# Which of a pair's two products with K gets which PSUM bank, in a fused attention kernel

## The chip, the cores and the metric

The kernel runs on one core of a Trainium2 chip. The metric is the device time of one execution in microseconds (us). The kernel before takes 1962.55 us (median of 3 runs, 1960.83 to 1966.76).

The engines in this text: PE is TensorE (PEld its weight loads), ACT is ScalarE, DVE is VectorE, POOL is GpSimd, SP issues most transfers. PE writes its results into PSUM, which has eight banks of 128 x 512 fp32 elements.

## What is computed

Two attention blocks read the same input x (2048 tokens, width 512, 32 heads of 16) and are mixed by a gate. Block A is causal within each of four segments of 512 tokens and adds a memory of the segments before; block B is full attention over 2048 keys.

```python
x = A_x
g = _sigmoid((x * gate_w).sum(-1, keepdims=True))
a = _A_ref(x, A_wq, A_wk, A_wv, A_wo, A_beta)
b = _B_ref(x, B_wqkv, B_wo)
return g * a + (1 - g) * b
...
scores = jnp.einsum("bhqd,bhkd->bhqk", q, k) * (Dh ** -0.5)
p = _softmax(scores, axis=-1)
o = jnp.einsum("bhqk,bhkd->bhqd", p, v)
...
logits = jnp.einsum("bhqd,bhkd->bhqk", qs, ks) * scale + mask
p = _softmax(logits, axis=-1)
a_dot = jnp.einsum("bhqk,bhkd->bhqd", p, vs)
```

## The kernel before

The first 336 us project q, k and v, build A's memory and begin with the running maxima. Then come 32 passes (the loop over `k`, line 919), one for each set of four heads and 512 queries. Each pass handles one unit of B (16 blocks of 128 keys) and one unit of A (4 blocks of 128 keys, below and on the diagonal).

**Groups.** A pass is cut into 37 groups (the loop over `n`, line 922): 32 for B, two heads of one key block each, then 5 for A. A group is one call of `t_group` (line 502) and consists of

- two products with K (line 514), one for each of two heads. Their results are 128 keys x 512 queries and each fills one PSUM bank. The two heads lie in rows 0 to 63 and 64 to 127, so that PE runs the two products side by side. A's last three groups have four smaller products, two in each bank;
- two exponentials on ACT (line 520), in the order of the products. Exponential `j` reads bank `bs[j]` whole and writes the probabilities to `raw`; for A, POOL then clears what lies above the diagonal (line 523).

**Banks.** `bank` (line 87) returns, of the banks that it may use, the one whose last *call* is longest ago. It keeps a list of calls and knows nothing of products or readers. `t_group` calls it twice (line 506). In passes 0 to 30 it may use three banks: two named `tb` and one named `mb`; so the calls of successive groups go A B, C A, B C, and so on. In pass 31 two more banks (`sbk`) are allowed. Twice in a pass another user takes a bank out of the same three: `m_rows` (line 483, the transposition of the maxima, PE line 487, behind group 24) and, from pass 9 on, `out_mm` (line 598, twelve products of the output projection, PE line 602, in group 1; pass 31 has a second one).

**The order of the work.** The schedule is written by hand, and each engine runs its instructions in the order of the program. Between the products of one group and those of the next, PE runs: the products for the running maxima of a later unit (`s_b`, line 453, two products into an `sbk` bank, read by a DVE reduction, line 462; or `s_a`, line 428, for A), and half of the products with V of the key block before (`pv`, line 526, eight products in most groups, all into bank `pvb`). In pass 0 groups 0, 2, 4 and 6 also hold one projection job each (`qk_job`, line 285). Behind the last group of every second pass from pass 8 on, ACT copies four blocks of the output (`out_split`, line 594). Results leave `pvb` once for each unit (`fin_copy`, line 539), and the divisions and the output follow in the next pass. Transfers are issued by SP in the order of the program.

Of the kernel before, what the change touches and what calls it, by code (L numbers as in the profile page):

```python
# [34 lines left out]
def gated_mix_kernel(ctx, tc, xt, wq, wk, wv, wo, beta, wqkv, wob, gate_w, out):  # L35
# [51 lines left out]
    def bank(allowed):  # L87
        b = min(allowed, key=lambda a: max([n for n, x in enumerate(lru) if x is a], default=-1))
        lru[:] = [x for x in lru if x is not b] + [b]
        return b  # L90
# [295 lines left out]
    def q_of(u):  # L386
        return QA[u % 2] if u < 32 else QB[u % 3]

    def k_of(u, p):
        return KA[u % 2][:, p] if u < 32 else KB[(u - 32) % 3][:, p]  # L390
# [111 lines left out]
    def t_group(u, n, banks):  # L502


        kd, qd, c = UN[u]
        bs = [bank(banks) for _ in range(2)]
        c0 = 0
        for it, hs in (((n // 2, (n % 2 * 2, n % 2 * 2 + 1)),) if kd == "B" else GA[n]):
            q0 = 128 * it if kd == "A" else 0
            w = C - q0  # L510
            pn = it if kd == "B" else it % 2
            for j, h in enumerate(hs):
                r = slice(64 * j, 64 * j + 64)
                nc.tensor.matmul(bs[j][:, c0:c0 + w], k_of(u, h // 2)[r, 128 * it:128 * it + 128],  # L514
                                 q_of(u)[r, h // 2, q0:], start=True, stop=True)
                PT[u, it, h] = PTILE[pn % 2][:, 2 + j if (kd, it) == ("A", 2) else h][:, c0:c0 + w]
            c0 += w
        for j in range(2):
            pt = PTILE[pn % 2][:, 2 + j if (kd, n) == ("A", 4) else hs[j]]
            nc.scalar.activation(pt, bs[j], AF.Exp, scale=SCALE)  # L520
            if kd == "A":
                m = pt[:, :128] if n < 2 else pt.rearrange("p (a t) -> p a t", a=4)[:, ::3 if n < 4 else 2]
                nc.gpsimd.affine_select(out=m, in_=m, pattern=[[1, 128]] if n < 2 else [[0, 2], [1, 128]],  # L523
                                        compare_op=OP.is_ge, fill=0.0, base=0, channel_multiplier=-1)
# [394 lines left out]
    for k in range(32):  # L919
        ua, ub = k, 32 + k  # L920
        banks = T3 + [b[:, 0] for b in SBK] * (k == 31)
        for n in range(NG):
            it = n // 2 if n < NG - 1 else NT + 2
            t_group(*(ub, n) if n < 2 * NT else (ua, n - 2 * NT), banks)
            for f in plan.get((k, n), []) + ex[k][0].get(n, []):
                f()
# [82 lines left out]
```

## Time and profile before

| | before |
|---|---|
| time, median of 3 runs | 1962.55 us |
| time of the profiled execution | 1963.14 us |
| its span, first to last instruction | 1961.4 us |
| busy: PE, DVE, ACT, POOL | 99%, 83%, 73%, 14% |
| mean granted clock of PE | 0.998 |
| first product of pass 0, of pass 31 | 336.7 us, 1890.3 us |

The profile belongs to one execution. A row of a group list gives line, engine, operation, output<-input, shapes and count; behind the bar the busy time in us, the mean of one in ns, the idle time of the engine before these instructions and what ended most of it. A row of the waits gives who waited for whom, the total in us, the number of waits and the longest. A row of the timeline gives start and length in us, engine, line, operation and names, the count where neighbours are merged, and in brackets the idle time of the engine before it and what ended it. Buffer numbers are left out of names, so both banks `tb` read as tb. A row of the chain that ended last gives start, length, engine and line. PE's ends are modelled, since matmuls are pipelined.

### The profile page before, as it was taken

The page shows a single profiled execution, that of the slowest core. Times are in us where ns is not written, and L with a number is a line of the kernel's source. Part 1 is how long each engine was busy: PE and PEld are TensorE (multiplying, and loading weights), DVE is VectorE, ACT ScalarE, POOL GpSimd, SP SyncE. Part 2 cuts the span into 40 slices and gives each one's busy share as a digit, 9 for nine tenths or more (in the row PEclk, how much of TensorE's full clock was granted, in tenths as well). Part 3 has the DMA queues.
Part 4 walks back from the last instruction along what each step waited for, and adds up shares of the span by engine and source line. Part 5 has one row for each costly group of instructions (what it writes and reads, how often), then busy time and mean ns, then how long its engine had stood idle before and what let it go on. Part 6 is the DMA issues. An engine that isn't in the chain of part 4 may idle for free.

```text
span 1961.4 us, 43525 instructions
## 1 busy us (share of the span) xinstructions
PE 1938.5 (99%) x17485; PEld 942.3 (48%) x17485; DVE 1629.3 (83%) x1800; ACT 1433.3 (73%) x2699; POOL 268.6 (14%) x483
## 2 busy tenths in 40 slices
PE   8999999999999999999999999999999999999999
PEld 6887776444344444444444444444444444444445
DVE  6135765899999999999999999999999999999942
ACT  4233332688888888888888888888888888888884
POOL 4101000012120101111111111010101010101022
PEclk9999999999999999999999999999999999999999
DMA  7666656644443445343444443445444443434111
GB/s 221 170 195 195 194 187 179 154 98 114 97 115 90 108 90 107 82 111 81 115 87 114 87 114 86 113 86 114 87 107 95 107 95 88 101 88 107 48 50 58
DMA packets 163534, 222.23 MB, mean 113 GB/s; under 512 B 39788, under 2 KB 90428, under 8 KB 157572
## 3 DMA queue, kind: packets, MB, share of 16 engines
q1 hardware_dynamic: 159284, 211.41, 43.4%
q0 software_dynamic: 2992, 7.77, 2.1%
q8 instruction: 138, 2.26, 0.5%
q14 instruction: 64, 0.52, 0.1%
q10 hardware_dynamic: 1056, 0.26, 0.1%
HBM read 147.95 MB, written 68.16 MB: 110 GB/s over the span
## 4 chain that ended last, share of the span: by engine, by line
PE 95%; DVE 3%; ACT 1%; DMA 0%; SPq 0%; issue 0%; DVEq 0%; ACTq 0%
PE pvb L536 33%; PE tb L514 17%; PE sbk L460 12%; PE mb L514 9%; PE tb L290 4%; PE sbk L438 3%; PE tb L602 2%; PE mb L290 2%; PE sbk L273 1%; PE tb L273 1%; PE sbk L442 1%; PE pvb L290 1%; DVE mxb L462 1%; PE mb L602 1%; PE mb L273 1%; PE pvb L273 1%
## 5 line engine op out<-in xcount | busy, mean ns | idle before, releaser
L462 DVE TENSOR_REDUCE mxb<-sbk 128x2 f32<-128x1024 f32 x1024 | 1222.1, 1222 | 69.3 <-PE sbk L460 65.0
L520 ACT ACTIVATE raw<-tb 128x512 f32<-128x512 f32 x1555 | 887.6, 598 | 157.2 <-PE tb L514 81.7
L536 PE MATMUL pvb<-raw,vb 128*17 128x256 f32 (+1 forms) x8072 | 639.3, 388 | 0.0
L520 ACT ACTIVATE raw<-mb 128x512 f32<-128x512 f32 x782 | 467.9, 598 | 81.0 <-PE tb L514 38.3
L514 PE MATMUL tb<-qb,xh 64*128 64x512 f32 x872 | 331.1, 494 | 1.7 <-ACT raw L520 1.7
L536 PEld LDWEIGHTS pvb<-raw,vb 128*17 128x17 f32 x8072 | 134.4, 95 | 341.6 <-issue 336.5
L460 PE MATMUL sbk<-xh,qb 64*128 64x512 f32 x1344 | 281.7, 396 | 4.5 <-DMA xh<-dB 2.6
L514 PE MATMUL mb<-qb,xh 64*128 64x512 f32 x445 | 220.5, 495 | 0.0
L523 POOL TENSOR_SCALAR_AFFINE_SELECT raw<-raw 128x256 f32<-128x256 f32 (+1 forms) x320 | 115.5, 361 | 713.0 <-ACT raw L520 705.0
L514 PEld LDWEIGHTS tb<-qb,xh 64*128 64x128 f32 x872 | 124.5, 183 | 179.6 <-issue 90.1
L514 PE MATMUL tb<-qb,kb 64*128 64x512 f32 x470 | 179.4, 495 | 1.3 <-DVE st L300 0.8
L446 DVE TENSOR_REDUCE mx<-sbk 128x2 f32<-128x768 f32 (+1 forms) x128 | 136.7, 1090 | 25.2 <-PE sbk L442 19.2
L460 PE MATMUL sbk<-kb,qb 64*128 64x512 f32 x704 | 146.3, 398 | 0.0
L460 PEld LDWEIGHTS sbk<-xh,qb 64*128 64x128 f32 x1344 | 138.7, 186 | 9.0 <-DVE mxb L462 4.3
L514 PEld LDWEIGHTS mb<-qb,xh 64*128 64x128 f32 x445 | 81.3, 183 | 95.2 <-issue 50.4
L514 PEld LDWEIGHTS tb<-qb,kb 64*128 64x128 f32 x470 | 68.2, 183 | 100.1 <-issue 53.1
L514 PE MATMUL mb<-qb,kb 64*128 64x512 f32 x234 | 116.0, 496 | 0.0
L576 POOL TENSOR_TENSOR o<-o,d 128x512 f32<-128x512 f32 x31 | 39.8, 1283 | 548.9 <-DMA d<-rd 486.0
L536 PE MATMUL pvb<-raw,va 128*17 128x256 f32 (+2 forms) x1280 | 94.7, 384 | 0.8 <-ACT pvs L545 0.8
L438 PE MATMUL sbk<-ka,qa 64*128 64x256 f32 (+3 forms) x512 | 89.8, 358 | 0.3
L297 ACT ACTIVATE st<-tb 128x512 fp32r<-128x512 f32 x33 | 19.7, 598 | 84.4 <-DVE phi L296 49.1
L514 PE MATMUL tb<-qa,ka 64*128 64x512 f32 (+3 forms) x339 | 79.6, 372 | 0.0
(280 smaller groups left out, 1839.8 us busy)
## 6 DMA issues: line engine op xcount, KB each, us to landing
xh<-dB SPq DMA_DIRECT2D x38, 512.0 KB
vb<-vdB SPq DMA_DIRECT2D x16, 1088.0 KB
dB<-st SPq DMA_DIRECT2D x64, 256.0 KB
dA<-st SPq DMA_DIRECT2D x64, 256.0 KB
pd<-pvs SPq DMA_DIRECT2D x64, 256.0 KB
kb<-dB SPq DMA_DIRECT2D x22, 512.0 KB
xh<-dB SPq DMA_DIRECT2D x38, 256.0 KB
qb<-dB SPq DMA_DIRECT2D x64, 128.0 KB
```

The lines of the kernel that those rows point to most:

```text
L273: nc.tensor.matmul(b, lhs, WV[wi][:, k, :], start=n == 0, stop=n == 11)
L290: nc.tensor.matmul(b, WS[ws][w][wi][:, k, :], (XH, XL)[xi][c][:, k, :], start=n == 0, stop=n == 11)
L438: nc.tensor.matmul(b[:, j, c0:c0 + n], q_of(u)[r, p, i * 128:(i + 1) * 128], k_of(u, p)[r, :n], start=True, stop=False)
L446: nc.vector.tensor_reduce(m[:, :, p, i], b[:, :, :n], axis=AX.X, op=OP.max)
L460: nc.tensor.matmul(b[:, j], q_of(u)[r, p, i * 128:(i + 1) * 128], k_of(u, p)[r, kc * C:(kc + 1) * C], start=True, stop=True)
L462: nc.vector.tensor_reduce(MXB[u][:, :, p, i, kc], b, axis=AX.X, op=OP.max)
L514: nc.tensor.matmul(bs[j][:, c0:c0 + w], k_of(u, h // 2)[r, 128 * it:128 * it + 128], q_of(u)[r, h // 2, q0:], start=True, stop=True)
L520: nc.scalar.activation(pt, bs[j], AF.Exp, scale=SCALE)
L523: nc.gpsimd.affine_select(out=m, in_=m, pattern=[[1, 128]] if n < 2 else [[0, 2], [1, 128]], compare_op=OP.is_ge, fill=0.0, base=0, channe ...
L536: nc.tensor.matmul(PVB[32 * h:32 * h + E + 1, q0 + lo:q0 + hi], vt[:, it, 4 * q + h, :], pt[:, lo:hi], start=it == 0 and lo == 0, stop=it ...
L576: nc.gpsimd.tensor_tensor(o, o, d, op=OP.mult)
L602: nc.tensor.matmul(b, (AT["oh"], AT["ol"])[oi][:, g, a], (AT["wh"], AT["wl"])[wi][:, g, a], start=n == 0, stop=n == 11)
```

## The change

One line of `t_group` is changed. `bank` is called twice as before, in the same order, and the list of the two banks is then reversed: the first product and the first exponential use the bank of the second call, the second product and the second exponential the bank of the first call. All 1184 calls of `t_group` do so. Nothing else is touched.

```diff
@@ -503,7 +503,7 @@


         kd, qd, c = UN[u]
-        bs = [bank(banks) for _ in range(2)]
+        bs = [bank(banks) for _ in range(2)][::-1]
         c0 = 0
         for it, hs in (((n // 2, (n % 2 * 2, n % 2 * 2 + 1)),) if kd == "B" else GA[n]):
             q0 = 128 * it if kd == "A" else 0
```

## The prediction

> **What bounds the kernel now.** I read the page's totals first, then the list of waits, then the timeline of a few groups, then the chain that ended last over one whole pass. "Product" below means a product with K (line 514), "exponential" the ACT instruction of line 520 that reads its bank.
>
> ```profile
> span 1961.4 us, 43525 instructions
> PE 1938.5 (99%) x17485; PEld 942.3 (48%) x17485; DVE 1629.3 (83%) x1800; ACT 1433.3 (73%) x2699; POOL 268.6 (14%) x483
> L462 DVE TENSOR_REDUCE mxb<-sbk 128x2 f32<-128x1024 f32 x1024 | 1222.1, 1222 | 69.3 <-PE sbk L460 65.0
> L520 ACT ACTIVATE raw<-tb 128x512 f32<-128x512 f32 x1555 | 887.6, 598 | 157.2 <-PE tb L514 81.7
> ```
>
> PE is busy 99% of the span, ACT 73%, and one exponential takes 598 ns. That alone would say: PE sets the time and ACT has room. The list of waits says how little room:
>
> ```profile
> PEld tb L514 <- ACT raw L520: 155.4, 371, 0.6
> PEld mb L514 <- ACT raw L520: 77.2, 182, 0.9
> ```
>
> 553 weight loads of products already have ACT's release as the last one. (The idle time in these rows counts the weight loader, which also idles while the products with V stream, so it is no PE loss.) The timeline shows the rotation. An "x2" row merges neighbours: the exponential of 1002.86 ends 0.59 later, at 1003.45, and the next one starts at 1003.53.
>
> ```profile
> 1001.77 0.18 PEld L514 LDWEIGHTS mb<-qb,xh 64*128 64x128 f32 x1 [0.42 <-issue]
> 1001.78 0.18 PEld L514 LDWEIGHTS tb<-qb,xh 64*128 64x128 f32 x1
> ...
> 1002.37 0.60 ACT L520 ACTIVATE raw<-mb 128x512 f32<-128x512 f32 x1 [0.22 <-PE tb L514]
> ...
> 1002.86 1.26 ACT L520 ACTIVATE raw<-tb 128x512 f32<-128x512 f32 x2
> 1003.00 0.18 PEld L514 LDWEIGHTS tb<-qb,xh 64*128 64x128 f32 x1 [0.42 <-ACT raw L520]
> ...
> 1003.02 0.18 PEld L514 LDWEIGHTS mb<-qb,xh 64*128 64x128 f32 x1
> ```
>
> The group at 1001.77 writes mb, then tb. Its first exponential reads mb until 2.97, its second reads tb until 3.45. The next pair starts at 3.00 with the other tb bank, which is free, and its second product enters mb at 3.02, 0.05 us after mb was read. So today a pair waits for the **first** exponential of the group before, and PE gets there 0.03 us after that exponential ends. The second exponential ends 0.45 us after the pair has started, and nobody waits for it. This overlap, the next pair under the second exponential, holds the period at PE's own length.
>
> **The change, part by part.** It adds and removes no instruction and no transfer; it exchanges the two banks of each call. The order in which the rotation hands out banks stays, because it follows the calls. With calls (A, B), (C, A), (B, C), the first product takes B, then A, then C. Bank A was in the group before the bank of the second product, since that exchange was made there too, so the **second** exponential read it. The second product gets a bank whose reader ended a group earlier.
>
> The wait is thus moved, from the end of exponential 1 to the end of exponential 2, and from the pair's second product to its first. Behind that product stand, in PE's order, its partner, the two products of the running maxima (line 460), the eight with V (line 536) and the next pair. DVE's reductions wait for the maxima, ACT waits for the pair itself. So product, exponential 1, exponential 2 and the next product become a ring with nothing under it. Once in each pass the kernel before already has this very wait: the transposition of the maxima (line 487) takes a bank out of turn, so the second product behind it meets a bank of the second exponential.
>
> ```profile
> 1017.93 0.18 PEld L514 LDWEIGHTS tb<-qb,xh 64*128 64x128 f32 x1 [0.42 <-ACT raw L520]
> ...
> 1018.96 0.59 ACT L520 ACTIVATE raw<-mb 128x512 f32<-128x512 f32 x1
> ...
> 1019.60 0.18 PEld L514 LDWEIGHTS mb<-qb,xh 64*128 64x128 f32 x1
> ```
>
> From the start of a pair (1017.93) to a product that waited for its second exponential (ends 19.55, released 19.60) is **1.67 us**. In parts: 0.53 from the product's start to exponential 1, 0.49 to the start of exponential 2, 0.59 until its end, 0.05 to the release. I take 1.67 as the ring. From above: in the first timeline, the pair at 1001.77 has its exponential at 1002.37, 0.60 later instead of 0.53. That occurs where the first product itself had no wait; under the change it always has one, so I take 0.53 and keep 0.60 as the bound, a ring of 1.74. From below: a release after 0.03 (PE's distance at 1003.00) gives 1.65.
>
> Now one whole pass on the chain that ended last (it runs on PE, so the pieces give PE's own pace):
>
> ```profile
> 1036.23 0.43 PE tb L514
> ...
> 1037.45 0.43 PE tb L514
> ...
> 1038.11 2.94 PE mb L602 x12
> 1041.04 0.43 PE tb L514
> 1041.47 0.23 PE sbk L460
> 1041.70 0.56 PE pvb L536 x8
> 1042.26 0.43 PE mb L514
> ...
> 1063.12 0.45 PE tb L514 x2
> ...
> 1064.54 0.43 PE mb L514
> ...
> 1068.22 0.43 PE mb L514
> ...
> 1069.67 0.43 PE mb L514
> ...
> 1071.10 0.42 PE tb L514
> ...
> 1078.45 0.42 PE tb L514
> ...
> 1079.87 0.43 PE tb L514 x2
> ...
> 1081.19 0.37 PE mb L514
> ...
> 1083.07 0.37 PE tb L514
> ...
> 1084.63 0.43 PE tb L514 x4
> ...
> 1086.46 0.42 PE mb L514
> ```
>
> A normal group is 0.43 + 0.23 + 0.56 = 1.22 us of PE. Numbering the 37 groups of the pass from 0, each is raised to 1.67 unless it is longer:
>
> - group 0: 1.22, so +0.45. Group 1 holds the twelve output products (2.94) and takes 3.59: nothing.
> - groups 2 to 19: 1063.12 − 1041.04 = 22.08 for 18, 1.227 each: 18 × 0.443 = +7.98.
> - group 20: 1.42, +0.25. Groups 21 to 23: 3.68 for three, +1.33.
> - group 24 (1.45) is followed by the transposition, which shifts the rotation: there the first product needs exponential 1 only, as today, so nothing. Group 25: 1.43, +0.24.
> - groups 26 to 31: 7.35 for six, +2.67.
> - the five A groups: 1.42 (+0.25), 1.32 (+0.35), 1.88 (0), 1.56 (+0.11), 1.83 (0).
>
> That is **+13.63 us** on a pass of 50.23; 33 of its groups are raised, about 1030 in the 31 passes. PE's work of 1.22 and DVE's reduction (1222 ns, one in most groups) both fit under 1.67, so nothing else is raised. Passes 1 to 30 at 13.63 give 409. Passes 1 to 8 have no output products, so their group 1 pays too: 8 × 0.44 = 3.5, together 413. Pass 0 has four projection jobs (`qk_job`, line 285) among its first groups, which cover the groups they stand in; I take 0.8 of a pass, +11 (bounds 0 and 14). Pass 31 has five banks, so a pair waits for exponentials two groups back and ACT is its limit: +5, between 0 (hidden) and 8 (the 0.49 between two exponentials for each of its 16 pairs of B groups).
>
> One piece of ACT work loses its cover:
>
> ```profile
> L595 ACT ACTIVATE oh<-o x12: 1058/1060/1062, 784.3 to 1890.1; 128x1024 fp32r<-128x1024 f32 x12
> ```
>
> This copy stands in ACT's queue behind the last exponential of a pass, where the ring leaves only 0.58 us until the next one (0.05 + 0.53): up to 0.48 is added, less the 0.1 by which ACT's instructions overlap and the slack of group 36. I take 12 × 0.25 = 3 (0 to 6). DMA issues on SP keep their places and gain time.
>
> Sum: 413 + 11 + 5 + 3 = 432. The profiled execution took 1963.1, of which 1.7 lie outside the span; 1963.1 + 432 = **2395 us**. It lies 0.6 above the median of the runs, too little to correct for.
>
> **The rivals.**
>
> *Not slower.* If the bank that the first product gets was read by exponential 1 after all (the exchange of one group undoing that of the next), the wait keeps its place, and the pair is no longer split as at 1003.00 and 1003.02. Some 14 groups of a pass would gain that 0.02: 14 × 31 × 0.02 = 9 us, so 1954. This is also the case that the change doesn't do what it says. It decides wherever exponential 2 ended before PE arrives; the rows show it ending 0.45 after. Against it stands the rotation, which follows the calls and not the products. Chance 0.03.
>
> *The weight load slips under the wait.* If the 0.18 us load is done while PE waits, the ring is 1.49 and about 1030 groups get 0.18 back: 2395 − 185 = 2210. Against it: the load at 1019.60 starts 0.05 after the release, so the wait holds the load too. Chance 0.04. The Trainium skill, page "TensorE: Matmul & The Clock Gate", Part 2, step 1, says that PE pulls weight loads ahead of running matmuls where the row groups don't conflict; the row shows this for no load that itself carries the wait.
>
> *PE's clock falls.* PE would now idle 0.45 of every 1.67 us. Idling has cost clock here (columns: stretch, length, busy time by engine, granted clock, DMA):
>
> ```profile
> 314.00:318.00 4.00, 1.39 (x9) 0.99 (x8) 0.69 (x1) 1.18 (x2) 0.00 (x0) 1.00 0.57 149
> 318.00:322.00 4.00, 4.00 (x17) 2.72 (x17) 3.12 (x4) 0.00 (x0) 0.45 (x1) 0.57 0.58 206
> 1900.00:1916.00 16.00, 16.00 (x102) 5.18 (x96) 2.71 (x9) 16.00 (x34) 0.00 (x0) 1.00 0.04 10
> ```
>
> PE was busy for 1.39 of 4 us, and in the next 4 us the clock was 0.57. At half clock PE's 1.22 becomes 2.44, which is longer than the ring: 0.77 more in each of 1030 groups, about 3200 us. Against it: the ring leaves PE busy for 73%, in pieces of 1.22, and in the ACT-bound stretch from 1900 on, with 102 matmuls in 16 us, the clock stayed 1.00. Chance 0.03. The same page, "A second HAM failure mode: psum-queue depth-cycling", warns of just this pattern: PE idling briefly at PSUM banks often enough to be throttled between bursts; the third row speaks against it here.
>
> **How the numbers follow.** The forecast has 0.90, the rivals 0.03, 0.04 and 0.03. Inside the forecast, the ring at 1.65 takes 0.02 × 1030 = 21 off, and the lower bounds of passes 0 and 31 some 15: 2359. At 1.74 it adds 0.07 × 1030 = 72 and the upper bounds 9; that end is the less likely one, and I stop at 1.73: 2465. These hold 0.85. What a measurement of this kernel can tell from no change is about 0.3%, or 6 us. Faster: the first rival, 0.02 of its 0.03; same: 0.01; slower: 0.97.
>
> **What would show it.** In the profile after: in the main passes the row of ACT's idle time before line 520, mostly behind PE, at about 0.6 us a group (1.67 less 1.08 of exponentials); first products starting 0.05 behind the end of the second exponential; the two products of a pair starting together; 1.67 from pair to pair; a pass of 64; DVE's and PE's true work unchanged with PE's busy share lower; the clock at 1.00; groups 1 and 24 as long as before. It is wrong if first products still start under the second exponential, if the ring is not 1.65 to 1.74, or if the clock falls.

## The result, and the profile after

| | before | after |
|---|---|---|
| time, median of 6 runs each | 1964.01 us | 2383.94 us |
| range of the runs | 1960.83 to 1966.76 | 2382.76 to 2385.66 |
| span of the profiled execution | 1961.4 us | 2381.8 us |
| ratio | | 1.214, 95% interval 1.213 to 1.216 |

The six runs before include the three quoted further up. The exchange costs 420 us. Rows of the page of the kernel after: the totals, the clock's line, the chain that ended last by engine, then the groups of DVE's reductions, of the exponentials and of the products with K into `tb`.

```profile
span 2381.8 us, 44001 instructions
...
PE 1986.9 (83%) x17485; PEld 923.5 (39%) x17485; DVE 1666.3 (70%) x1800; ACT 1437.4 (60%) x2699; POOL 267.9 (11%) x483
...
PEclk9999999999999999999999999999999999999999
...
PE 48%; ACT 31%; issue 19%; DVE 1%; DMA 0%; SPq 0%; ACTq 0%; DVEq 0%
...
L462 DVE TENSOR_REDUCE mxb<-sbk 128x2 f32<-128x1024 f32 x1024 | 1252.1, 1225 | 408.8 <-PE sbk L460 406.0
L520 ACT ACTIVATE raw<-tb 128x512 f32<-128x512 f32 x1555 | 884.8, 595 | 436.5 <-PE tb L514 272.9
...
L514 PE MATMUL tb<-qb,xh 64*128 64x512 f32 x872 | 326.9, 495 | 153.1 <-ACT raw L520 152.1
```

The work is what it was: as many matmuls, exponentials and reductions. The busy shares fell because the span grew. Two idle times grew together: ACT's before the exponentials of `tb`, from 157.2 to 436.5 us, of which 272.9 behind products into `tb` (81.7 before), and PE's before these products, from 1.7 to 153.1, of which 152.1 behind ACT. Two engines that each idle behind the other point to a ring, and the chain that ended last shows it: ACT stands in it with 31%. DVE's idle time grew as well, from 69.3 to 408.8, but it is fed later and holds nobody up: the waits of PE and its weight loads for DVE's reductions come to under 6 us in the whole run. Before, the chain's row and that of the same products read

```profile
PE 95%; DVE 3%; ACT 1%; DMA 0%; SPq 0%; issue 0%; DVEq 0%; ACTq 0%
...
L514 PE MATMUL tb<-qb,xh 64*128 64x512 f32 x872 | 331.1, 494 | 1.7 <-ACT raw L520 1.7
```

The timeline of a normal stretch (start, length, engine, line, names; in brackets the idle time and what ended it):

```profile
1240.28 0.50 PE L514 MATMUL tb<-qb,xh 64*128 64x512 f32 x1 [0.39 <-ACT raw L520]
...
1240.28 0.50 PE L514 MATMUL mb<-qb,xh 64*128 64x512 f32 x1
...
1240.81 0.60 ACT L520 ACTIVATE raw<-tb 128x512 f32<-128x512 f32 x1 [0.58 <-PE mb L514]
...
1241.30 0.59 ACT L520 ACTIVATE raw<-mb 128x512 f32<-128x512 f32 x1
1241.94 0.18 PEld L514 LDWEIGHTS mb<-qb,xh 64*128 64x128 f32 x1 [0.88 <-ACT raw L520]
1241.95 0.49 PE L514 MATMUL mb<-qb,xh 64*128 64x512 f32 x1 [0.39 <-ACT raw L520]
...
1241.95 0.49 PE L514 MATMUL tb<-qb,xh 64*128 64x512 f32 x1
```

The second exponential reads mb until 1241.89. The next pair's first product goes into that same mb, and its load starts 0.05 later. From pair to pair it is 1241.95 − 1240.28 = 1.67 us. The tb of the last row was free all the time and could not be used, since its product stands behind in PE's order. PE idles 0.39 in each ring and ACT 0.58.

Whole passes, by stretches (length, then busy time of PE, PEld, DVE, ACT, POOL, granted clock, DMA share and GB/s): pass 0, pass 14 and pass 31 to the end, first after, then before.

```profile
335.64:408.51 72.87, 62.48 (x546) 28.82 (x546) 55.30 (x54) 43.93 (x82) 5.83 (x14) 1.00 0.56 135
1223.31:1287.09 63.78, 52.08 (x508) 20.98 (x504) 47.83 (x48) 40.99 (x77) 7.42 (x14) 1.00 0.39 89
2309.24:2381.80 72.56, 65.74 (x392) 33.23 (x388) 21.89 (x53) 42.72 (x87) 12.90 (x22) 1.00 0.15 50
```

```profile
336.72:399.94 63.22, 61.62 (x545) 29.05 (x544) 54.49 (x54) 43.89 (x82) 5.82 (x14) 1.00 0.62 152
1036.16:1086.39 50.23, 50.22 (x510) 21.30 (x506) 46.80 (x48) 40.93 (x77) 7.47 (x14) 1.00 0.47 113
1890.32:1961.40 71.08, 66.31 (x392) 34.69 (x388) 21.87 (x53) 42.01 (x87) 12.88 (x22) 0.99 0.16 51
```

Pass 14 grew by 13.55, pass 0 by 9.65, pass 31 with the tail by 1.48. Passes 1 to 30 together: from 408.51 to 2309.24 is 1900.73, from 399.94 to 1890.32 was 1490.38, so +410.35. The stage before pass 0 ended 1.1 earlier. The sum is 420.4, the whole difference of the spans.

### The profile page after: what moved, and what is told of

The parts are those of the page before. It is cut to its first block, busy times and chain, and to the rows that moved or that the text cites. A ratio compares the mean times of both kernels' runs of the same rounds, so it can differ in the third digit from the quotient of the medians.

```text
span 2381.8 us, 44001 instructions
## 1 busy us (share of the span) xinstructions
PE 1986.9 (83%) x17485; PEld 923.5 (39%) x17485; DVE 1666.3 (70%) x1800; ACT 1437.4 (60%) x2699; POOL 267.9 (11%) x483
## 4 chain that ended last, share of the span: by engine, by line
PE 48%; ACT 31%; issue 19%; DVE 1%; DMA 0%; SPq 0%; ACTq 0%; DVEq 0%
ACT raw L520 30%; PE tb L514 17%; PE mb L514 9%; PE tb L290 4%; PE pvb L536 3%; PE tb L602 2%; PE mb L290 2%; PE sbk L438 1%; PE sbk L273 1%; PE tb L273 1%; PE pvb L290 1%; PE sbk L460 1%; PE mb L602 1%; PE mb L273 1%; PE sbk L442 1%
## 5 line engine op out<-in xcount | busy, mean ns | idle before, releaser
L462 DVE TENSOR_REDUCE mxb<-sbk 128x2 f32<-128x1024 f32 x1024 | 1252.1, 1225 | 408.8 <-PE sbk L460 406.0
L520 ACT ACTIVATE raw<-tb 128x512 f32<-128x512 f32 x1555 | 884.8, 595 | 436.5 <-PE tb L514 272.9
L514 PE MATMUL tb<-qb,xh 64*128 64x512 f32 x872 | 326.9, 495 | 153.1 <-ACT raw L520 152.1
L460 PE MATMUL sbk<-xh,qb 64*128 64x512 f32 x1344 | 272.8, 393 | 2.9 <-DMA xh<-dB 2.2
L460 PEld LDWEIGHTS sbk<-xh,qb 64*128 64x128 f32 x1344 | 133.0, 186 | 6.2 <-issue 2.7
L514 PEld LDWEIGHTS mb<-qb,kb 64*128 64x128 f32 x234 | 42.8, 183 | 99.1 <-ACT raw L520 95.1
```

Of the source, the lines that this page charges most:

```text
L460: nc.tensor.matmul(b[:, j], q_of(u)[r, p, i * 128:(i + 1) * 128], k_of(u, p)[r, kc * C:(kc + 1) * C], start=True, stop=True)
L462: nc.vector.tensor_reduce(MXB[u][:, :, p, i, kc], b, axis=AX.X, op=OP.max)
```

## The experiments

Three questions were put: is it the order of reading that decides, and not the bank by itself; does the ring hide PE's work, and is the second exponential in it; and what does a pair that waits for the first exponential really cost?

**Banks exchanged, and the order of reading too.**

```diff
-        bs = [bank(banks) for _ in range(2)]
+        bs = [bank(banks) for _ in range(2)][::-1]
...
-        for j in range(2):
+        for j in (1, 0):
             pt = PTILE[pn % 2][:, 2 + j if (kd, n) == ("A", 4) else hs[j]]
```

> The exchanged banks, and the two exponentials of a group in the other order as well, so that the bank which the next first product takes is read first again. Theory (the ring runs through whichever exponential reads the first product's next bank): the pair waits for the first exponential as in the kernel before; ring 0.53 + 0.60 + 0.05 = 1.18, under PE's 1.22; 1955 to 1965 us. Rival (the exchange of banks itself costs, whoever reads them): stays at about 2384.

Measured: 1983.07 us, ratio 1.010 (1.008 to 1.011). Of the 420 us 19 are left: the banks are those of the slow kernel, and only the order in which ACT reads them differs. That settles the question between reader and bank. The number itself missed the range by 18. The timeline of this run shows why:

```profile
1057.82 0.49 PE L514 MATMUL tb<-qb,xh 64*128 64x512 f32 x1
...
1058.42 0.60 ACT L520 ACTIVATE raw<-mb 128x512 f32<-128x512 f32 x1 [0.16 <-PE mb L514]
...
1059.07 0.18 PEld L514 LDWEIGHTS mb<-qb,xh 64*128 64x128 f32 x1 [0.46 <-ACT raw L520]
```

The first exponential starts 0.60 behind the pair and not 0.53, so the ring is 0.60 + 0.60 + 0.05 = 1.25. That is above PE's 1.22. Group by group against the trace before, the groups that took 1.22 pay 0.03 and those that took 1.24 pay 0.01; in passes 1 to 30 this is 18 and 3 us, and groups 24 and 25 together add 3. The first exponential now reads the second product's bank, and that product's load carries no wait. The last run below takes this up.

**Only the order of reading.** The edit of the exponentials' loop alone, with the banks of the kernel before.

> The banks as in the kernel before, only the two exponentials of a group in the other order. Theory: the second product now waits for the bank that was read last, and the exponential that is queued first needs that second product, so the ring is the same 1.67: 2384, within 20. Rival (the exchange of banks costs): as the kernel before, 1964. Rival (a wait of the second product is cheaper, as its partner has started): between, about 2100.

Measured: 2391.0 us, ratio 1.218 (1.216 to 1.220): 427 us above the kernel before (1963.95), so about the same loss with the banks untouched. The timeline of this run:

```profile
1242.50 0.49 PE L514 MATMUL mb<-qb,xh 64*128 64x512 f32 x1
1242.95 0.18 PEld L514 LDWEIGHTS tb<-qb,xh 64*128 64x128 f32 x1 [0.27 <-ACT raw L520]
...
1243.48 0.60 ACT L520 ACTIVATE raw<-tb 128x512 f32<-128x512 f32 x1 [0.58 <-PE sbk L460]
...
1243.98 0.59 ACT L520 ACTIVATE raw<-mb 128x512 f32<-128x512 f32 x1
...
1244.62 0.18 PEld L514 LDWEIGHTS mb<-qb,xh 64*128 64x128 f32 x1 [0.27 <-ACT raw L520]
```

The first product starts early, at 1242.50, and gains nothing: the exponential that is first in ACT's queue needs the second product, which waits for the bank that was read last (released at 1242.95, then 1244.62, again 1.67). PE waits in the middle of the pair instead of ahead of it.

**The banks exchanged in odd groups only.**

```diff
-        bs = [bank(banks) for _ in range(2)]
+        bs = [bank(banks) for _ in range(2)][::1 - 2 * (n % 2)]
```

> The banks exchanged in every second group only (odd groups of a pass). Theory: the odd group's first product takes the bank that was read first, the even group's second product one that was read last; the ring of 1.67 closes in every second group and the other one keeps PE's 1.22, so 2.89 for two groups and half of the loss: about 2180, within 30. Rival (only the group that is exchanged counts, not what was done in the group before): no loss when the neighbour is not exchanged, 1964; or the full 2384.

Measured: 2171.1 us, ratio 1.105 (1.103 to 1.107), half of the loss. The timeline of this run, even groups at 1147.65 and 1150.54, an odd one at 1149.32:

```profile
1147.65 0.50 PE L514 MATMUL tb<-qb,xh 64*128 64x512 f32 x1
1148.11 0.18 PEld L514 LDWEIGHTS mb<-qb,xh 64*128 64x128 f32 x1 [0.27 <-ACT raw L520]
...
1149.32 0.50 PE L514 MATMUL tb<-qb,xh 64*128 64x512 f32 x2
...
1150.54 0.49 PE L514 MATMUL mb<-qb,xh 64*128 64x512 f32 x1
1150.99 0.18 PEld L514 LDWEIGHTS tb<-qb,xh 64*128 64x128 f32 x1 [0.27 <-ACT raw L520]
```

From 1147.65 to 1150.54 is 2.89, as expected. The group at 1149.32 starts both products at once; the groups at 1147.65 and 1150.54 are split: their second product starts 0.45 behind the first, because it waits for the second exponential of the group before. What counts is a group's assignment together with that of the group before it.

**More work for PE, in both kernels.** The two products of the running maxima are issued twice for B's units 34 to 63, with the same values.

```diff
         b = rot("s", SBK)
-        for j in (1, 0):
+        for j in (1, 0) * (1 + (u > 33)):
             r = slice(64 * j, 64 * j + 64)
```

> The exchanged banks, and in units 34 to 63 of B the two products for the running maxima are issued twice (the same values into the same bank): 960 times 0.23 us of PE more. Theory: PE idles about 0.45 in each ring, so it is hidden except in groups 1 and 24, which don't wait for the ring: 2384 + 2 x 30 x 0.23 = 2398, within 10. Rival (PE still sets the time, at a lower rate or clock): 2384 + 221 = 2605.

> The kernel before with the same doubled products. Theory: there PE sets the time and pays for them: 1964 + 960 x 0.23 = 2185, within 25. Rival (ACT's ring sets the time in the kernel before too): about 1975.

Measured: with the exchanged banks 2396.08 us, 12 above the kernel without this work (2383.94); in the kernel before 2160.21 us, ratio 1.101 (1.099 to 1.103), 198 above its 1962.3. The same 1920 products cost 198 us where PE sets the time and 12 where the ring does. The 198 lie at the lower edge of what was expected: the groups that took 1.22 before grew by 0.23 and those of 1.24 by 0.21, but groups 20 and 25, which took over 1.4, hardly grew. The timeline of the former run shows them under the ring:

```profile
1244.23 0.49 PE L514 MATMUL tb<-qb,xh 64*128 64x512 f32 x1 [0.15 <-ACT raw L520]
...
1244.57 0.62 PE L460 MATMUL sbk<-kb,qb 64*128 64x512 f32 x4
...
1245.90 0.49 PE L514 MATMUL mb<-qb,xh 64*128 64x512 f32 x1 [0.16 <-ACT raw L520]
```

Four products instead of two, PE's idle time 0.15 instead of 0.39, and the ring still 1.67.

**A shorter second exponential, in both kernels.** The second exponential of B's groups handles the first 256 of its 512 columns, so half of these heads' probabilities are not computed.

```diff
-            nc.scalar.activation(pt, bs[j], AF.Exp, scale=SCALE)
+            e = 256 if j and kd == "B" else 512
+            nc.scalar.activation(pt[:, :e], bs[j][:, :e], AF.Exp, scale=SCALE)
```

> The exchanged banks; the second exponential of B's groups reads and writes 256 of its 512 columns, so part of the probabilities is left out. Theory: its length stands in the ring; 256 columns fewer are about 0.21 us less (an estimate: 598 ns for 512 columns, most of it per column), ring 1.46, some 900 raised groups: 2384 - 190 = 2194, within 30. Rival (the pair still waits for the first exponential, or PE's clock or the bank costs): 2384, less at most 20 in pass 31.

> The kernel before with the same shorter second exponential, the same part left out. Theory: nobody waits for the second exponential but the product behind group 24 and pass 31, where ACT sets the time: 1964 - 13 = 1951, between 1945 and 1964. Rival (ACT's total is what counts): 1024 x 0.21 less, about 1750.

Measured: 2184.8 us with the exchanged banks, 199 less than with the whole exponential; 1953.35 us in the kernel before, ratio 0.995 (0.994 to 0.997), 9 less. So the length of the second exponential is in the ring after the change, and before it hardly anything waits for it. The 9 us lie where they were expected: 6.0 at group 25, whose 1.44 became 1.22 (it follows the transposition), and 3.4 in pass 31. The timeline with the exchanged banks (the exponentials' line is 521 here):

```profile
1201.38 0.49 PE L514 MATMUL tb<-qb,kb 64*128 64x512 f32 x1 [0.18 <-ACT raw L521]
...
1202.84 0.49 PE L514 MATMUL mb<-qb,kb 64*128 64x512 f32 x1 [0.17 <-ACT raw L521]
```

The ring is 1.46 us, 0.21 shorter.

**One fixed bank for the first product.** In passes 0 to 30 the first product always takes the same bank, whose reader is the first exponential, and the second product alternates between the other two.

```diff
-        bs = [bank(banks) for _ in range(2)]
+        bs = [bank(banks[:1]), bank(banks[1:])] if len(banks) == 3 else [bank(banks) for _ in range(2)]
```

> The kernel before, but in passes 0 to 30 the first product always takes the same bank and the second product alternates between the other two; the exponentials in the order of the products. The first product's load then carries the wait for the first exponential of the group before, in every group. Theory (a first exponential starts 0.53 behind its product when that product's load itself waited for ACT, and 0.60 when it did not and the exponential carries a second wait): ring 0.53 + 0.60 + 0.05 = 1.18 everywhere, under PE's 1.22, so the groups of 1.24 become 1.22: 1964 - 9 = 1955, between 1950 and 1962. Rival (the 0.60 in the run with both orders exchanged came from the exchanged order of reading): the groups stay at 1.22 and 1.24, 1964. Rival (a pair whose first product waits has no free product to start early and loses PE time): 1983 as in that run.

Measured: 1952.05 us, ratio 0.995 (0.994 to 0.997) to the kernel before, so half a per cent faster than it: a small gain, but the interval excludes equality. Its timeline:

```profile
1043.09 0.50 PE L514 MATMUL tb<-qb,xh 64*128 64x512 f32 x2
...
1043.62 1.82 ACT L520 ACTIVATE raw<-tb 128x512 f32<-128x512 f32 x3
...
1044.31 0.50 PE L514 MATMUL tb<-qb,xh 64*128 64x512 f32 x1
...
1045.53 0.50 PE L514 MATMUL tb<-qb,xh 64*128 64x512 f32 x2
```

The pair at 1043.09 has its exponential at 1043.62, 0.53 behind, and the pairs come 1.22 apart in even and odd groups alike; the kernel before alternated between 1.22 and 1.24 in most of its groups. That agrees with the first of the three expectations: a first exponential starts 0.53 behind its product where that product's load carried the wait for ACT, and 0.60 where the exponential has a waiting instruction of ACT's queue ahead of itself. Counted over the 960 B groups of passes 1 to 30 in the traces: with such an instruction ahead of the first exponential the median is 0.59 (420 groups of the kernel before, 30 after the change, 30 here) or 0.60 (870 groups of the run with both orders exchanged); without it 0.53 (540, 930, 930) or 0.55 (90). The semaphores on record in the trace of the kernel before say what this instruction does: it waits for a count that PE alone raises and starts 0.53 to 0.54 behind the product; the exponential starts 0.06 later and itself waits for a count of ACT's own (390 groups) or of POOL's (30). Without it, the exponential waits for PE's count itself.

## Why the prediction was right

Time: 2395 was forecast and 2384 measured, in the range. By the steps of the prediction:

- **The wait moves to the second exponential.** Right, by the timeline after (load 0.05 behind the end of the exponential). The run with both orders exchanged shows that the reader decides, the one with odd groups that the neighbour's assignment belongs to it.
- **The ring of 1.67**, read before the change from the one place in a pass where a product already met it. Right to the hundredth. The choice of 0.53 against 0.60 was right too, for the reason given: the first product now carries the wait, and 930 of the 960 groups counted have 0.53.
- **PE's and DVE's work fits under the ring.** Right: 198 us of PE work shrank to 12.
- **Groups 1 and 24 stay.** Right: in pass 14 group 1 took 3.60 before and after. Group 24 after the change:

```profile
1265.34 0.50 PE L514 MATMUL tb<-qb,xh 64*128 64x512 f32 x1 [0.39 <-ACT raw L520]
...
1266.37 0.59 ACT L520 ACTIVATE raw<-mb 128x512 f32<-128x512 f32 x1
...
1266.76 0.50 PE L514 MATMUL tb<-qb,xh 64*128 64x512 f32 x1
...
1267.01 0.50 PE L514 MATMUL mb<-qb,xh 64*128 64x512 f32 x1
```

  1.42 from group 24 to 25, with 1.45 before, and the partner at 1267.01 starts 0.05 behind the end of the second exponential (1266.96), as the shifted rotation says.
- **Passes 1 to 30: +413, and 3 for the copies of the output.** Measured +410.35 for both, 5.7 less: the largest miss of the sum. Pass 14 grew by 13.55 instead of 13.63; in it group 34 was put at nothing and got 0.14 shorter. The copies took about 1 of their 3: from pass 9 on a pass that begins behind a copy takes 64.01 and one without 63.79 (medians), where before it was 50.37 and 50.24. One more us is in pass 3, which took 48.95 before where its neighbours took 47.9.
- **Pass 0: +11.** Measured 9.65, within its bounds of 0 and 14.
- **Pass 31: +5 of 0 to 8.** Measured 1.48 for the pass with its tail. With five banks and ACT as the limit (it was busy for 15.89 of the 16 us from 2320 to 2336) most of the later product starts were hidden. This makes 3.5 of the 12 us between the forecast rise (432) and the measured one (420). The rest is 1.3 of pass 0 and the 1.1 by which the stage ahead of it was shorter, which the sum didn't have.
- **The rivals.** Not slower: excluded by the time and by the timeline, where the wait stands behind the second exponential. Its price was put too high: it counts some 14 groups of a pass that take 1.24, and the trace before has ten. The weight load under the wait: excluded, since the load starts only at 1241.94, 0.05 behind the end of the exponential, and the ring is 1.67 and not 1.49. The clock: 1.00 in the three passes after. The Trainium skill, page "TensorE: Matmul & The Clock Gate", "A second HAM failure mode: psum-queue depth-cycling", tells of a kernel in which PE's clock oscillates because it idles briefly and often as it goes through its banks; here it idled 0.39 us in each ring for 1900 us and the clock stayed at 1.00, so this trace shows no such thing for gaps of this size.

## What to carry to other kernels

Where pairs share three banks as here, the bank that is handed out again first should be the one that was read first; look at the order in which the reader's queue empties the banks, not only at how long ago a bank was handed out. A wait that the trace showed in one odd place (behind the transposition) was here a free measurement of what it would cost everywhere. In this kernel it also paid to put the wait on the product whose exponential comes first: one bank kept for the first product, and two that alternate for the second, took half a per cent off the kernel before.

## What was not expected

That a first exponential starts 0.06 to 0.07 us later when a waiting instruction of ACT's queue stands ahead of it, and that this is enough to lift a ring of 1.18 above PE's 1.22. The fixed bank gained 9.5 us, about the 9 that were expected from groups of 1.24 that become 1.22, but in part by luck. The trace before has ten such groups in a pass, not the 14 behind that estimate, and in passes 1 to 30 they gave 6 us. Another 3 came from groups 20 and 32, which went from 1.42 to 1.36 and which nobody had counted. The run with both orders exchanged has the 0.60 in nearly every group and was 19 us slower than the kernel before, where equality had been expected.
